# Linear attention and channel mix on one core: a new instruction order, late gate and output tiles in the two-bank PSUM tiles, weight loads as a chain of their own

## The chip, the core and the metric

The kernel runs on one NeuronCore of a Trainium2 chip. The metric is the device time of one execution in microseconds (us). Five runs of the kernel before gave 278.98, 279.91, 278.3, 282.97 and 279.36; their median is 279.36. The profiled execution took 278.98 us, and its span, from the first to the last instruction, is 277.2 us.

Five engines work in parallel, each through its own queue in its own order: PE (matmuls), DVE (vector), ACT (activation functions), POOL (GpSimd) and SP (here only DMA issues). An instruction whose input is not there blocks everything behind it in its engine's queue.

## The reference

Two stages follow each other. The first is a linear attention with a learned feature map, over 8 batches, 8 heads, 576 positions and head dimension 64:

```python
def phi(x):
    proj = einsum('bhsd,df->bhsf', x, w_phi)            # 128 features
    proj = proj - max(abs(proj), axis=-1)
    return concatenate([exp(proj), exp(-proj)], axis=-1)
q_p, k_p = phi(q), phi(k)
kv  = einsum('bhsf,bhsd->bhfd', k_p, v);  z = sum(k_p, axis=2)
num = einsum('bhsf,bhfd->bhsd', q_p, kv)
den = einsum('bhsf,bhf->bhs', q_p, z) + 1e-6
attn = num / den
```

Its output, laid out as 8 x 576 x 512, goes through a channel mix:

```python
x_prev = x shifted by one position (zeros first)
xk = mu_k * x + (1 - mu_k) * x_prev
xr = mu_r * x + (1 - mu_r) * x_prev
k = maximum(xk @ w_k, 0)                                # 512 -> 1024
out = sigmoid(xr @ w_r) * ((k * k) @ w_v)               # 1024 -> 512
```

## The kernel before

**Units of work.** Attention goes by pairs of heads: four pairs in each batch, 32 in all, numbered n = 0 to 31 (pair n belongs to batch n // 4). The channel mix goes by batches b = 0 to 7: the first 512 positions of a batch in `add_moe`, the last 64 positions of two neighbouring batches together in `add_moe_edge`, numbered 0 to 3.

**Steps of a pair** (`add_pair`), each a named operation on one engine:

- `kp`, `qp` (PE, L566) project keys and queries; `rk`, `rq` (DVE, L579 and L584) take the maximum of the absolute values over features.
- `ea`, `eb` (ACT, L605) are the exponentials of the keys; `em` (ACT, L591) those of the maxima; `va`, `vb` (L597, POOL or DVE) scale the values by them.
- `mh`, `mt`, `mc` bring the query maxima into transposed form; `qt` (PE) projects the queries a second time, transposed, and adds the maxima; `qa`, `qb` (ACT, L643) are the exponentials.
- `kv` (PE, L656) sums keys times values, `kc` copies it; `nd` (PE, L677) gives numerator and denominator; `ra`, `rd` (DVE, L685 and L689) divide.
- For pairs 0 to 7 `xt` (PE, L715) transposes the result and `xe`, `xf` copy it; from pair 8 on `xz` does it as a DMA transpose on SP's queue, and `xu` patches the edge.
- `df`, `xa`, `xb` (L726, L732) form the shifted difference and the two mixes xk and xr.

The last 64 positions of each batch go through a smaller set (`add_edge`: `tp`, `rt`, `mhe`, `mte`, `mce`, `qte`, `eme`, `ekt`, `eqe`); `tp` (PE, L466) reads the transposed inputs of all four pairs of its batch.

**Steps of a batch in the channel mix:** `h` (PE, L810, eight per batch, four matmuls each) with `rl` (relu) and `sq` (square); `r` (PE, L829, four per batch) with `th` (tanh, ACT); `v` (PE, L843, four per batch, eight matmuls each) with `ob` (DVE, L849) and `so` (two output DMAs). The edge has `he`, `re`, `ve`, `obe`, `soe`.

An `h` of batch b needs the four `xa` of that batch, an `r` its four `xb`, a `v` all eight `sq` and the weight `w_v`.

**Loads.** Keys and queries of a batch come by `lk` and `lq`, DMAs on POOL's queue that also convert to bf16 (the first pair of batch 0 instead by `hk`, `hq` on SP and ACT, with copies named `lk0.0.d`, `lq0.0.d`). Values come by `lv`, on POOL or SP. In batches 0 and 1 PE transposes keys and queries (`pt`, copied by `pa` and `pb`); from batch 2 on `tr` does it, two DMA transposes per batch on SP's queue (L352), named `tr2.0`, `tr2.2` and so on. The weights come in two DMAs each on POOL's queue: `wk.0`, `wk.1`, `wr.0`, `wr.1`, `wv.0`, `wv.1` (L432). `mus` loads mu_k and mu_r.

**PSUM.** Eight banks are held as three tiles of two banks each (tags P0 to P2, `ptile`) and two tiles of one bank (M0, M1, `motile`). Attention's large results use P tiles. All results of the channel mix and the small transposes use M0 and M1.

**Order.** Every operation is registered with `op(...)`, with its engine, an estimated length, dependencies, and the buffers that it takes and frees. None of these numbers has an effect in this file: the order in which the operations are issued is written out in the string `ORDER`, the result of a planner that ran elsewhere. A word is `name:i/ENGINE+n@t`: `:i` is the PSUM tile, `/ENGINE` the engine where there is a choice, and `+n@t` puts n idle matmuls on a tile of ones ahead of it (`fill`, L292; they compute nothing that is used and keep PE busy). Each engine gets its own operations in the order of this string; waits follow from the data.

Of the kernel before, what the change touches and what calls it, by code (L numbers as in the profile page):

```python
# [19 lines left out]
ones hk hq ident dve2 hk.d hq.d wphi wphi.d lk0.1 lk0.1.d lq0.1 lq0.1.d mus mus.d lk0.2 lk0.2.d dve3  # L20
lq0.2 lq0.2.d lv0.0/POOL lv0.0.d lk0.0.d/DVE lq0.0.d/ACT lv0.1/SP lv0.1.d pt0.0:0+9@0 lv0.2/SP
lv0.2.d pt0.1:1 pa0/DVE pb0/ACT tr0 dve1 tp0.0:0+1@2 kp0:1 rt0.0 qp0:2 rk0 eme0.0 mhe0.0/POOL ekt0.0
pt1.0:1+1@0 lk1.0 lk1.0.d pa1/ACT mte0.0:0 rq0 ea0 lq1.0 lq1.0.d pt1.1:1+2@2 pb1/DVE tr1 lk1.2
lk1.2.d eb0 kp1:2+2@2 tp0.1:0 lq1.2 lq1.2.d rt0.1 em0 rk1 qp1:1+1@1 ekt0.1 mh0/POOL eme0.1 wk.0
wk.0.d mt0:1+1@1 mc0/ACT mce0.0/DVE rq1 ea1 qt0:0+1@2 wk.1 wk.1.d wk.d pt2.0:1 qa0 pt2.1:0
mhe0.1/DVE mh1/POOL pa2/DVE pb2/DVE tr2 eb1 vb0/POOL pt3.0:1+2@3 pt3.1:0 pa3/DVE qb0 pb3/DVE tr3
va0/POOL mte0.1:1+1@3 qp2:2 mt1:0 rq2 qp3:1 mce0.1/ACT mc1/ACT em1 qte0.1:1 wr.0 wr.0.d qt1:0 eqe0.1
qte0.0:0 rq3 lv1.0/POOL lv1.0.d qa1 tp0.2:2 va1/POOL qb1 rt0.2 kp2:1+3@1 rk2 vb1/POOL ekt0.2
kv0:0+1@1 eqe0.0 pt4.0:1 kc0/DVE ea2 mhe0.2/POOL pt4.1:0 pa4/DVE kp3:0 pb4/DVE tr4 kv1:2 wr.1 wr.1.d
wr.d eb2 rk3 pt5.0:0 wv.0 wv.0.d pt5.1:1 eme0.2 qp4:1 pa5/DVE kc1/ACT mh2/POOL em2 rq4 nd0:2  # L30
mh3/POOL pb5/ACT tr5 wv.1 wv.1.d wv.d em3 mt2:0 pt6.0:1 ea3 mc2/DVE ra0 nd1:1 vb2/POOL pa6/DVE rd0
eb3 pt6.1:0 pt7.0:1 va2/POOL pb6/DVE tr6 qt2:2 pa7/ACT ra1 rd1 mte0.2:0 qa2 lk2.0 lk2.0.d pt7.1:1
mce0.2/DVE qp5:0 pb7/DVE tr7 qte0.2:0 lq2.0 lq2.0.d qb2 rq5 tp1.0:1 xt0:1 va3/POOL eqe0.2 kv2:2
rt1.0 xf0/ACT xe0/ACT kp4:0 mh4/POOL mt3:0 kc2/ACT rk4 xt1:1 df0/POOL mc3/ACT ekt1.0 nd2:2 ra2 ea4
vb3/POOL xe1/DVE qt3:1+1@0 rd2 mt4:0 xf1/ACT mc4/ACT df1/DVE qa3 xt2:1 xa0 kv3:2 eb4 mhe1.0/DVE
xe2/DVE mte1.0:0+1@0 xb0 kc3/ACT kp5:0 qb3 qt4:2 xa1 eme1.0 xf2/DVE nd3:1 rk5 mce1.0/ACT df2/POOL
qa4 ra3 qb4 rd3 lv1.2/POOL lv1.2.d ea5 xa2 xt3:0+7@1 qp6:2 xb1 qte1.0:1 xe3/ACT qp7:1 eb5 xf3/DVE
df3/DVE xa3 em4 qt5:0+1@0 eqe1.0 rq6 vb4/POOL h0.0:0 qa5 va4/POOL rq7 kp6:2 qb5 h0.1:1 rk6 mh6/POOL
kp7:1 rl0.1/ACT kv4:0 va5/POOL rl0.0/ACT tr2.0 tr2.0.d tr8 tr9 mt6:1 kc4/DVE ea6 h0.2:0 rk7 vb5/POOL
eb6 xb2 kv5:0+1@2 mc6/ACT sq0.0/ACT xb3 nd4:2 tr2.2 tr2.2.d tr10 tr11 em6 ea7 h0.3:1 kc5/DVE  # L40
vb6/POOL ra4 rd4 nd5:0 eb7 vb7/POOL rl0.3/DVE qt6:2 rl0.2/ACT ra5 qp8:1 rd5 qa6 lv2.0/SP lv2.0.d
sq0.1/POOL r0.0:1 rq8 qb6 va6/POOL qp9:0 h0.4:0 rq9 th0.0 sq0.3/POOL sq0.2/ACT qt7:2 kv6:1 rl0.4/DVE
qa7 lk3.0 lk3.0.d tp2.0:0 kc6/DVE h0.5:1 mh8/POOL rt2.0 qb7 va7/POOL xt4:0 rl0.5/ACT kp8:1 xf4/DVE
xe4/DVE qp10:2 eme2.0 lq3.0 lq3.0.d r0.1:1 rk8 ekt2.0 mhe2.0/POOL r0.2:0 th0.1 rq10 sq0.4/POOL ea8
kp9:0 h0.6:1 rk9 lv2.2/POOL lv2.2.d eb8 kv7:2 th0.2 df4/DVE qp11:1 sq0.5/DVE rl0.6/ACT h0.7:0 xa4
em8 sq0.6/ACT kc7/DVE va8/POOL mt8:1 rq11 rl0.7/ACT nd6:2 mc8/ACT ea9 mte2.0:0 vb8/POOL xt5:1 ra6
nd7:1 rd6 tr3.0 tr3.0.d tr12 tr13 mce2.0/ACT eb9 vb9/POOL qte2.0:0 ra7 kv8:2 rd7 xf5/ACT sq0.7/ACT
qt8:0 va9/POOL kc8/DVE eqe2.0 kp10:1 xe5/DVE kp11:2 rk10 v0.0:1 tr3.2 tr3.2.d tr14 tr15 df5/POOL qa8
rk11 ea10 lk4.0 lk4.0.d v0.1:0 qb8 mh10/DVE xa5 lv3.0/SP lv3.0.d eb10 xb5 kv9:0 xb4 em10 qt9:1
kc9/ACT ob0.0 va10/POOL nd8:0 qa9 ob0.1 v0.2:1 qb9 vb10/POOL ra8 rd8 ea11 lq4.0 lq4.0.d mt10:0  # L50
tp3.0:0 ob0.2 kv10:1 mc10/ACT vb11/POOL eb11 rt3.0 so0.2 so0.2.d xt6:0 xt7:1 kc10/ACT va11/POOL
kp12:2 xf7/ACT xf6/DVE qt10:1 xe6/DVE ekt3.0 xz8 xz8.d xe7/DVE r0.3:0 df6/DVE qa10 rk12 df7/POOL
nd9:0 qb10 v0.3:1 ra9 mhe3.0/POOL rd9 th0.3 xa6 ea12 xz9 xz9.d mte3.0:0 qt11:0 xa7 eb12 nd10:1
mce3.0/DVE ob0.3 tr4.0 tr4.0.d tr16 tr17 h1.0:0 qa11 xb6 h1.1:1 qb11 ra10 xb7 kv11:2 rl1.0/ACT rd10
kp13:0 eme3.0 tr4.2 tr4.2.d tr18 tr19 sq1.0/POOL qte3.0:0 kc11/DVE rl1.1/ACT qp12:1 rk13 qp13:2
# [105 lines left out]
def kernel(  # L161
# [21 lines left out]
    DM = moe_mu_k.shape[0]  # L183
# [36 lines left out]
    op = plan.op  # L220
# [796 lines left out]
```

## Time and profile before

| what | value |
|---|---|
| median of five runs | 279.36 us |
| profiled execution | 278.98 us |
| its span | 277.2 us |
| PE busy | 264.9 us |
| DVE busy | 234.6 us |
| ACT busy | 223.1 us |
| POOL busy | 142.6 us |
| granted TensorE clock | 0.999 |
| DMA | 42.89 MB, mean 155 GB/s |

Busy time is the time in which at least one instruction of the engine was running. For PE the ends of matmuls are modelled and overlap, so its busy time says that matmuls were in flight and not that the array was full. In brackets behind an instruction the profile gives the idle time of its engine before it, and what ended it.

### The profile page before, as it was taken

The page shows a single profiled execution, that of the slowest core. Times are in us where ns is not written, and L with a number is a line of the kernel's source. Part 1 is how long each engine was busy: PE and PEld are TensorE (multiplying, and loading weights), DVE is VectorE, ACT ScalarE, POOL GpSimd, SP SyncE. Part 2 cuts the span into 40 slices and gives each one's busy share as a digit, 9 for nine tenths or more (in the row PEclk, how much of TensorE's full clock was granted, in tenths as well). Part 3 has the DMA queues.
Part 4 walks back from the last instruction along what each step waited for, and adds up shares of the span by engine and source line. Part 5 has one row for each costly group of instructions (what it writes and reads, how often), then busy time and mean ns, then how long its engine had stood idle before and what let it go on. Part 6 is the DMA issues. An engine that isn't in the chain of part 4 may idle for free.

```text
span 277.2 us, 8913 instructions
## 1 busy us (share of the span) xinstructions
PE 264.9 (96%) x3730; PEld 154.3 (56%) x3730; DVE 234.6 (85%) x388; ACT 223.1 (80%) x413; POOL 142.6 (51%) x193
## 2 busy tenths in 40 slices
PE   7999889999599999999999999999999999999993
PEld 3567656565355566555565665555566565444542
DVE  5899999999599989999999889998889797764222
ACT  3899999999599997789898999789987876626330
POOL 6799557976528764534459664830930621300200
PEclk9999999999999999999999999999999999999999
DMA  7999999599999999879799999982635234143034
GB/s 152 269 208 251 208 206 180 124 230 156 214 152 209 199 188 147 180 162 226 92 188 154 193 240 148 184 218 101 144 104 88 64 64 99 35 110 73 22 93 115
DMA packets 65817, 42.89 MB, mean 155 GB/s; under 512 B 47152, under 2 KB 57008, under 8 KB 65776
## 3 DMA queue, kind: packets, MB, share of 16 engines
q1 hardware_dynamic: 54496, 27.54, 49.7%
q0 software_dynamic: 11056, 14.42, 30.3%
q8 instruction: 29, 0.48, 0.7%
q10 hardware_dynamic: 224, 0.36, 0.5%
q14 instruction: 12, 0.10, 0.1%
HBM read 33.62 MB, written 9.44 MB: 155 GB/s over the span
## 4 chain that ended last, share of the span: by engine, by line
PE 81%; DVE 7%; ACT 6%; DMA 4%; issue 1%; SPq 0%; ACTq 0%
PE ps_h L810 20%; PE ps_v L843 18%; PE ps_r L829 10%; PE ps_nd L677 6%; PE ps_kv L656 5%; DMA qkT<-nat 4%; PE ps_he L897 3%; PE ps_k L566 3%; PE ps_ve L929 3%; PE ps_q L566 3%; PE ps_qT L630 2%; PE ps_qT L636 2%; ACT k L605 2%; DVE nmk L579 2%; PE ps_f L292 1%; DVE nmq L584 1%
## 5 line engine op out<-in xcount | busy, mean ns | idle before, releaser
L597 POOL TENSOR_TENSOR v<-vt,v 128x576 bf16<-128x576 f32 x59 | 69.8, 1202 | 30.8 <-ACT v L591 28.4
L605 ACT ACTIVATE k<-ps_k 128x1024 bf16<-128x1024 f32 x64 | 64.8, 1047 | 1.3 <-DVE nmk L579 1.3
L643 ACT ACTIVATE q<-ps_qT 128x1024 bf16<-128x1024 f32 x64 | 63.9, 1054 | 1.8 <-PE ps_qT L636 1.7
L810 PE MATMUL ps_h<-xk,wk_bf 128*128 128x512 bf16 x256 | 61.7, 380 | 0.1
L843 PE MATMUL ps_v<-wv_bf,kk 128*128 128x512 bf16 x256 | 59.0, 379 | 0.0
L579 DVE TENSOR_REDUCE nmk<-ps_k 128x8 f32<-128x1024 f32 x32 | 38.8, 1217 | 1.8 <-PE ps_k L566 1.5
L584 DVE TENSOR_REDUCE nmq<-ps_q 128x8 f32<-128x1024 f32 x32 | 38.3, 1217 | 1.6 <-PE ps_q L566 1.4
L843 PEld LDWEIGHTS <-kk 128*128 128x128 bf16 x256 | 24.1, 98 | 27.3
L810 PEld LDWEIGHTS <-wk_bf 128*128 128x128 bf16 x256 | 22.7, 98 | 25.0 <-issue 0.7
L206 ACT ACTIVATE krelu<-ps_h 128x512 bf16<-128x512 f32 x48 | 28.8, 611 | 9.3 <-PE ps_h L810 9.3
L726 POOL TENSOR_TENSOR diff<-xs 128x576 bf16<-128x576 bf16 x15 | 20.2, 1345 | 30.2 <-ACT xs L706 12.8
L214 POOL TENSOR_TENSOR kk<-krelu 128x512 bf16<-128x512 bf16 x18 | 19.1, 1068 | 30.3 <-ACT krelu L206 26.6
L849 DVE SCALAR_TENSOR_TENSOR ob<-rt,ps_v 128x512 f32<-128x512 bf16 x32 | 21.7, 682 | 14.3 <-PE ps_v L843 13.4
L829 PE MATMUL ps_r<-wr_bf,xr 128*128 128x512 bf16 x128 | 32.0, 380 | 0.0
L732 DVE SCALAR_TENSOR_TENSOR xk<-diff,mu_k_t,xs 128x576 bf16<-128x576 bf16 x32 | 26.7, 839 | 0.1
L835 ACT ACTIVATE rt<-ps_r 128x512 bf16<-128x512 f32 x32 | 19.7, 615 | 8.8 <-PE ps_r L829 8.7
L689 DVE TENSOR_TENSOR x_sc<-ps_nd,rden 128x640 bf16<-128x640 f32 x32 | 26.0, 817 | 0.6
L732 DVE SCALAR_TENSOR_TENSOR xr<-diff,mu_r_t,xs 128x576 bf16<-128x576 bf16 x32 | 25.6, 806 | 0.1
L656 PE MATMUL ps_kv<-v,k 64*128 64x65 bf16 x1024 | 22.5, 190 | 0.3 <-ACT q L643 0.2
L566 PEld LDWEIGHTS <-qkT 64*128 64x128 bf16 x512 | 16.5, 94 | 11.0 <-issue 8.0
L656 PEld LDWEIGHTS <-k 64*128 64x128 bf16 x1024 | 19.3, 94 | 5.7 <-issue 1.8
L677 PE MATMUL ps_nd<-kv,q 128*128 128x65 bf16 x512 | 21.4, 193 | 0.0
(102 smaller groups left out, 415.5 us busy)
## 6 DMA issues: line engine op xcount, KB each, us to landing
out_dram<-ob SPq DMA_DIRECT2D x70, 128.0 KB, 2.5
vt<-in_v_dram SPq DMA_DIRECT2D x11, 576.0 KB, 5.6
nat<-in_k_dram POOLq DMA_DIRECT2D x6, 576.0 KB, 9.2
nat<-in_q_dram POOLq DMA_DIRECT2D x6, 576.0 KB, 9.1
vt<-in_v_dram POOLq DMA_DIRECT2D x4, 576.0 KB, 6.1
wk_bf<-in_moe_w_k_dram POOLq DMA_DIRECT2D x2, 512.0 KB, 12.1
wv_bf<-in_moe_w_v_dram POOLq DMA_DIRECT2D x2, 512.0 KB, 11.1
nat<-in_k_dram POOLq DMA_DIRECT2D x3, 288.0 KB, 7.0
```

Of the source, the lines that this page charges most:

```text
L566: nc.tensor.matmul(ps[:, par, g * 128:(g + 1) * 128], lhsT=qkT[b][r, g0 + gg + g, :], rhs=wph[r, :], start=(g == 0), stop=(g == 3))
L579: nc.vector.tensor_reduce(t[:, j, :], s["k"].rearrange("p a (g f) -> p (a g) f", f=128), axis=AX.X, op=ALU.max, apply_absolute_value=True, ...
L584: nc.vector.tensor_reduce(t[:, j, :], s["q"].rearrange("p a (g f) -> p (a g) f", f=128), axis=AX.X, op=ALU.max, apply_absolute_value=True, ...
L597: (nc.vector if eng == "DVE" else nc.gpsimd).tensor_tensor(vb[:, a, pn, :, 0:64], vt[b, a // 2][:, a % 2, :].rearrange("p (s d) -> p s d", ...
L605: nc.scalar.activation(s[f"k{pn}"], s["k"].rearrange("p a (g f) -> p (a g) f", f=128), AF.Exp, scale=(1.0 if pn == 0 else -1.0))
L643: nc.scalar.activation(t.rearrange("f x (a p) -> f x a p", a=2), s["qT"].rearrange("f a (x p) -> f x a p", p=64), AF.Exp, scale=(1.0 if pn ...
L656: nc.tensor.matmul(ps[:, hh, pn * 65:(pn + 1) * 65], lhsT=s[f"k{pn}"][r, c, :], rhs=vb[r, a, pn, 2 * g + par, :], start=(pn == 0 and c == ...
L677: nc.tensor.matmul(ps[:, bk, o * 65:(o + 1) * 65], lhsT=tail if sl < 2 else s[f"q{pn}"][:, 2 * G + h, :], rhs=s["kv"][:, h, pn, :], start= ...
L732: nc.vector.scalar_tensor_tensor(out=t[:, a, (b % 2) * S:(b % 2 + 1) * S], in0=s["d"], scalar=mu[:, a:a + 1], in1=xs[:, a, 0:S], op0=ALU.m ...
L810: nc.tensor.matmul(ps, lhsT=wk_bf[:, c, fc * 128:(fc + 1) * 128], rhs=xkt[bp][:, c, m0:m0 + 512], start=(c == 0), stop=(c == NDC - 1))
L829: nc.tensor.matmul(ps, lhsT=xrt[bp][:, c, m0 + ci * 128:m0 + (ci + 1) * 128], rhs=wr_bf[:, c, :], start=(c == 0), stop=(c == NDC - 1))
L843: nc.tensor.matmul(ps, lhsT=s["kk"][:, fc, ci * 128:(ci + 1) * 128], rhs=wv_bf[:, fc, :], start=(fc == 0), stop=(fc == NFC - 1))
```

## The change

Three things change in the code, and the string `ORDER` is replaced as a whole.

1. In `add_moe` and `add_moe_edge` the results of `r`, `v`, `re` and `ve` of batches 6 and 7 (and of the last edge) take the first bank of a P tile; for batches 0 to 5 they stay in M0 and M1. `h` and `he` stay in M tiles throughout.

```diff
+    def ntile(key, name):
+        return motile(key, name) if key[0] == "mo" else ptile(key, name)[:, 0, :]
...
+    LATE = 6
...
+        rv = "mo" if b < LATE else "P"
...
-                s["r", ci] = ps = motile(("mo", f"r{b}.{ci}"), "ps_r")
+                s["r", ci] = ps = ntile((rv, f"r{b}.{ci}"), "ps_r")
...
-                s["v", ci] = ps = motile(("mo", f"v{b}.{ci}"), "ps_v")
+                s["v", ci] = ps = ntile((rv, f"v{b}.{ci}"), "ps_v")
```

2. The weight loads get a planner chain of their own; `chain` is not read in this file, and shows only in the order.

```diff
-            op(f"{nm_}.{i}", "POOL", 0.75, i - 8, ldw(...), ["ident"], chain="ld")
+            op(f"{nm_}.{i}", "POOL", 0.75, i - 8, ldw(...), ["ident"], chain="w")
```

3. Of the four output DMAs of the last edge, two instead of one are issued from ACT.

```diff
-                e = "ACT" if hf == 1 and i == 1 else "SP"
+                e = "ACT" if i == 1 else "SP"
```

4. The order. The operations are the same; their places, PSUM tiles and, where there is a choice, engines differ throughout. The places that the prediction speaks of, by engine (before, then after):

```diff
 POOL, from the start
-ident lk0.1 lq0.1 lk0.2 lq0.2 lv0.0 mhe0.0 lk1.0 lq1.0 lk1.2 lq1.2 mh0 wk.0 wk.1 mh1 vb0 va0 wr.0 lv1.0
-va1 vb1 mhe0.2 wr.1 wv.0 mh2 mh3 wv.1 vb2 va2 lk2.0 lq2.0 va3
+ident lv0.1 lk0.1 lq0.1 lk0.2 lq0.2 lv0.2 lk1.0 lq1.0 lk1.2 lq1.2 mhe0.0 wk.0 mh0 va0 vb0 mhe0.1 wk.1
+mh1 lk2.0 mh2 vb1 va1 lv1.0 mhe0.2 lq2.0 wr.0 va2 mh3 vb2 va3 wr.1 vb3
 POOL, around the loads of batch 3
-vb5 vb6 vb7 sq0.1 va6 sq0.3 lk3.0 mh8 va7 lq3.0 mhe2.0 sq0.4 lv2.2
+va5 lk3.0 mh6 vb5 vb6 lq3.0 va6 sq0.2 wv.0 wv.1 vb7 sq0.4 va7
 SP, from the start
-hk wphi mus lv0.1 lv0.2 tr2.0 tr2.2 lv2.0 tr3.0 tr3.2 lv3.0
+hk lv0.0 wphi mus tr2.0 lv1.2 tr2.2 lv2.0 tr3.0 tr3.2 lv2.2 xz8 lv3.0
 DVE, from the start
-ones dve2 dve3 lk0.0.d pa0 dve1 rt0.0 rk0 rq0 pb1 rt0.1 rk1 mce0.0 rq1 mhe0.1 pa2 pb2 pa3 pb3 rq2
+ones dve2 dve3 lq0.0.d pa0 dve1 rt0.0 rk0 pa1 rq0 rk1 mc0 rq1 pa2 pb2 rt0.1 pa3 rq2 pb3 rk2
 PE, the last words
-h7.7 he3.0 v6.3 v7.0 he3.1 r7.2 r7.3 v7.1 v7.2 v7.3 re3 ve3.0 ve3.1
+h7.7 r6.3 r7.0 he3.0 r7.1 r7.2 v7.0 he3.1 v7.1 r7.3 v7.2 v7.3 re3 ve3.0 ve3.1
 output DMAs at the end
-SP: soe3.0.a soe3.0.b soe3.1.a          ACT: soe3.1.b
+SP: soe3.1.a soe3.0.a                   ACT: soe3.0.b soe3.1.b
 idle matmuls in all
-36
+30
```

Between the first `h` of batch 0 (`h0.0`) and the first of batch 1 (`h1.0`) PE's list holds the same operations as before and four more: `kp13`, `qp12`, `kv11` and `qte3.0`, which before stood behind `h1.0`.

## The prediction

> **What bounds the kernel now.** I read the busy time by stage first, cut at the moments that the order makes important: the last `xa` of batch 0 (39.9), the first long wait (69), the start of `h1.0` (80.3), the last matmul (273). Columns: stage, length, then busy time of PE, PEld, DVE, ACT and POOL with instruction counts, clock, DMA share, GB/s.
>
> ```profile
> 0.00:39.90 39.90, 35.27 (x561) 22.65 (x562) 35.59 (x77) 34.02 (x75) 29.11 (x50) 1.00 1.10 221
> 39.90:69.00 29.10, 28.43 (x525) 17.32 (x526) 28.82 (x43) 28.61 (x51) 23.56 (x28) 1.00 0.98 167
> 69.00:80.30 11.30, 8.50 (x142) 5.28 (x141) 8.10 (x16) 8.49 (x14) 5.88 (x7) 1.00 1.29 204
> 80.30:273.00 192.70, 192.67 (x2510) 109.07 (x2506) 161.67 (x254) 151.95 (x277) 84.05 (x110) 1.00 0.71 138
> ```
>
> Two regimes: up to 80 DVE and ACT are the full engines (in the second stage DVE idles 0.28 us); from 80.3 PE has 0.03 us of gaps in 192.7, so nothing that frees a buffer there can gain. The stage between shows a hole on every engine. The chain of waits names it (start, length, what):
>
> ```profile
> 63.73 9.78 DMA qkT<-nat
> 73.51 0.05 issue
> 73.56 0.29 PE ps_e L466 x4
> ```
>
> `tp3.0` needs both DMA transposes of batch 3; `tr3.2`, issued at 63.73, lands 9.78 later. PE queues `kv10`, `xt6`, `kp12` behind it. DVE's timeline shows the cost, and where it idles early (idle time in brackets):
>
> ```profile
> 6.26 0.49 DVE L202 COPY qkT<-ps_pt 128x640 bf16<-128x640 bf16 x1 [1.39 <-PE ps_pt L338]
> 7.42 0.42 DVE L472 TENSOR_REDUCE me<-ps_e 128x2 f32<-128x256 f32 x1 [0.53 <-PE ps_e L466]
> 73.89 1.23 DVE L472 TENSOR_REDUCE me<-ps_e 128x8 f32<-128x1024 f32 x1 [2.67 <-PE ps_e L466]
> ```
>
> `h1.0` starts at 80.34, 0.33 after `xa7` ends on DVE (80.01). So the path is: DVE from the start to `xa7`, then PE to 272.97, then 4.22 of output to 277.19; outside the span the execution has 278.98 - 277.19 = 1.8.
>
> **The change, part by part.**
>
> *Start on DVE.* DVE is busy 35.59 of the 39.90 up to `xa3`, so 4.3 idle, nearly all before 16 us. In the new order its list up to `xa3` has the same reductions and mixes. Small copies change engine: `pa1`, `pa7`, `pb5`, `kc2`, `xe0`, `df2` and five shorter ones come (3.2 us), `pb1`, `xe1`, `xe2`, `df1`, `mhe0.1`, `mhe1.0` and five shorter ones go (3.0; 0.36 to 0.40 for a PSUM copy, 0.30 for a pair of small ones, start to start in the trace): 35.9. What changes is the idle time. Two value loads of 288 KB now go out ahead of keys and queries: `lv0.0` in SP's queue before `wphi` and `mus`, `lv0.1` in POOL's before `lk0.1`, `lq0.1`, `lk0.2`, `lq0.2`. In the trace these four land at 5.33, 6.87, 9.26 and 12.36; the first two are 1.55 apart for 288 KB. Lower bound of the delay: 0, if the values move before POOL's first packets (3.9 us). Upper: 2 x 1.55 = 3.1. I take one load, 1.55, halfway, because `lv0.1` stands in front of the keys in the same queue, while `lv0.0` follows `hk` (landed 4.39) in a queue that then carries only the small `wphi` and `mus`. `lq0.2` then lands at 13.9, `pt2.0` (five transposes, 0.45, and two hand-overs of 0.1) lets `pa2` start at 14.6. DVE's work ahead of `pa2` sums to 9.6 (three 1.13 reductions, 1.13 for `rk0`, 5.1 of set-up and copies), so idle is 5.0, with the bounds 3.5 and 6.5. `wphi` behind `lv0.0` delays `dve1` and `rk0` by up to 1; that lies inside the same idle time, since `pa2` waits anyway. `xa3` ends at 35.9 + 5.0 = 40.9 (39.4 to 42.4), against 39.90.
>
> POOL now issues ten loads in a row (about 0.75 each in the rows of its issues) before `mhe0.0`, which moves from 7.91 to 9.0; behind it `mte0.0`, `mce0.0` and then all of ACT's exponentials wait, `ea0` by 1.3. I cost this at nothing: ACT's list up to `qb5` is 2.0 shorter than before (32.7 against 34.7), and `qb3`, which feeds DVE's `ra3`, comes at 31 while DVE reaches `ra3` at 35. Without that cover it would be 1.3.
>
> [...]
>
> *Middle on DVE.* From `xa3` to `xa7` DVE needed 80.01 - 39.90 = 40.1: 36.3 of work, 2.67 + 0.42 in the hole, 0.7 in small gaps. The new list has 2.0 more work before `xa7` (`ob0.3` 0.60, `ra10` + `rd10` 0.95, `sq0.0`, `sq0.3`, `sq0.6` 1.02, small ones; less `rl0.4`, two copies of kv and others). `lk3.0` and `lq3.0` pass `vb5`, `vb6`, `vb7`, `sq`, `va7` on POOL (1.1 us each) and so go out some 7 us earlier; before they were issued at 51.8 and 54.2 and landed 5.8 and 6.3 later. With `lq3.0` issued at 47 and landed by 54, `tr3.2` is issued by 57 and lands, at the same 9.8, by 67; `tp3.0` is reached at about 67. I take the hole as gone, bounds 0 and 3.1 left. `lv2.2` now waits in SP's queue behind `tr3.2`: issued at 60 instead of 56.4, at its 6.8 it lands at 67, when POOL reaches `va10` (67.4 before), so nothing. `lk2.0` and `lq2.0` too come earlier, but before nothing waited for `tr2`: nothing. So `xa7` ends at 40.9 + 38.3 + 0.7 = 79.9. PE has cover for this: its work from `h0.0` to `h1.0` is 32.9 before and 34.2 now (the four operations moved ahead), and in the 40.5 it took before, 3.0 were the hole and 4.6 losses, so it needs 38.8 of the 39.1 there are. `h1.0` starts at 80.0.
>
> *The end on PE.* Before, `h1.0` to the last matmul took 192.6: 184.4 at the shortest start-to-start times of each operation (`h`, `r` 0.863, `v` 1.726, `nd` 0.635, `kv` 0.555, `qt` 0.43, `kp`, `qp` 0.233) and 8.2 on top. Of that 6.9 are 68 changes between 64-row and 128-row matmuls at 0.1 each. The new order leaves 183.0 behind `h1.0` and has 66 changes: 191.1 with the rest unchanged. Last matmul at 271.1; bounds of new stalls 0 to 3, taken 0, since DVE's list runs some 4 us ahead of PE at `h3.0` by the sums of both.
>
> *P tiles for the last `r` and `v`.* The last stretch before:
>
> ```profile
> 251.09 6.95 PE ps_h L810 x32
> 258.04 0.89 PE ps_he L897 x16
> 258.93 3.45 PE ps_v L843 x16
> ```
>
> 32 matmuls in 6.95 are 217 ns each, the same as in a single group: with two M tiles nothing waits. The matmuls are the same, so gain 0 (at most 0.6, all of the excess after 240), loss at most 1 where the new `h7.0`, now ahead of `v6.0`, meets `xa31`, which by DVE's list ends about 1 us before it.
>
> *Idle matmuls.* Six fewer (0.45 each in the first nine): PE waits there for DVE in any case, so 0; 2.7 at most if it did not.
>
> *Output at the end.* SP issues `soe3.0.a` after `soe3.1.a`, 0.54 each, both behind `obe3.1`; ACT takes one more. Last issue at 1.1 instead of 0.95 after `obe3.1`: +0.2, so 4.4.
>
> Sum: 271.1 + 4.4 + 1.8 = **277.3 us**, 0.6% under the profiled execution (278.98) and 0.7% under the median (279.36).
>
> [...]
>
> **The rivals.**
>
> *A. The late weights take the place of the hole (slower).* `wv.0` and `wv.1` move on POOL from 21 and 23 us to behind `lq3.0` and `sq0.2`, about 51. The six weight rows land 8.9 to 13.0 after issue: 60 to 64.4. `v0.0` comes on PE at 40.9 + 19.2 + 3.7 = 63.8. If POOL, which before waited up to 7.6 for ACT ahead of a `va` or `vb`, reaches `wv.1` 4 later, it lands at 68.4, and `v0.0`, with `kp11`, `v0.1`, `tp3.0` behind it, loses 4.6: 281.9. It decides the sign once `wv.1` lands 3.5 after `v0.0`'s turn. Against it: DMA is less full there (share 0.98, against 1.10 early).
>
> *B. The start keeps what the middle gives (no change).* Both value loads in full and some more early waits: idle 7.5 instead of 5.0, 279.8. For it: DMA share 1.10 up to 40. Against it: most of the first 4 us of the queues are open.
>
> *C. The new order stalls PE after 80.* Ten hand-overs of 0.2 to 0.3 that the old order did not have: 2.5, 279.8. For it: every neighbour in the queues is new. Against it: DVE and ACT are idle for 31 and 41 us in that stage.
>
> **How the numbers follow.** Forecast 0.50, A 0.18, B 0.18, C 0.14. The forecast's own range is 275.8 to 278.9 (idle 3.5 to 6.5). Up to 0.5% either way (277.96 to 280.76) cannot be told from no change. Faster: 0.46 from the forecast, 0.02 each from B and C: 0.50. Slower: 0.15 from A, 0.04 from B, 0.05 from C: 0.24. Same: 0.26. The range is 275.6 to 281.0: below it 0.05, above it 0.14, most of A.
>
> **What would show it.** Right: no DMA wait at `tp3.0`, `h1.0` at 79 to 81.5, PE without gaps from there, 191 us to its last matmul. The start is read at `xa3` (40.9) and in DVE's idle time before `pa2`. Wrong: a wait of `v0.0` on `wv`, `xa3` after 43, PE gaps above 0.3 after 85, or the 9.8 of `tr3.2` back in the chain.

## The result and the profile after

| what | before | after |
|---|---|---|
| median of all runs, us | 281.08 (80 runs) | 281.26 (43 runs) |
| ratio after / before, 95% interval | | 1.0082 [1.0065, 1.0100] |
| profiled execution, us | 278.98 | 281.12 |
| its span, us | 277.2 | 279.3 |
| `xa3` ends | 39.90 | 41.27 |
| `xa7` ends | 80.01 | 83.29 |
| `h1.0` starts | 80.34 | 83.33 |
| last matmul ends | 272.97 | 275.01 |
| DVE standing still behind POOL ahead of `h1.0` (see below) | 0.00 | 3.94 |

The change made the kernel 0.8% slower; the forecast was 277.3 us, 0.6% faster. The ratio leaves out, for each kernel, the runs more than 1.5% above its fastest (in the changed kernel at a mean granted clock of 0.982 to 0.990, the others at 0.984 to 1.0), and the medians hold them, which is why the two medians lie so close.

The stages first, cut at the same events as before: end of `xa3`, 69, start of `h1.0`, last matmul (columns as in the prediction).

```profile
0.00:41.27 41.27, 32.69 (x558) 21.40 (x559) 36.63 (x75) 33.56 (x73) 30.17 (x53) 1.00 1.07 210
41.27:69.00 27.73, 25.54 (x489) 15.45 (x488) 27.06 (x42) 25.93 (x45) 22.42 (x27) 1.00 1.05 181
69.00:83.30 14.30, 12.88 (x235) 8.07 (x233) 14.20 (x24) 12.66 (x20) 8.48 (x6) 1.00 0.93 179
83.30:275.00 191.70, 190.88 (x2450) 107.68 (x2446) 161.67 (x246) 151.54 (x276) 83.59 (x112) 1.00 0.71 137
```

The hole of the third stage is gone: DVE is busy 14.20 of 14.30 us, where it had 8.10 of 11.30. Yet the first three stages together are 3.0 us longer. So DVE was kept busy and had more to be busy with; but 24 instructions in 14.20 us (0.59 each) against 16 in 8.10 (0.51) suggests that some of them became longer. DVE's timeline of after shows which (start, length, engine, line, operation; from the loads on, its line numbers are 3 to 6 higher than in before).

```profile
69.04 0.81 DVE L736 SCALAR_TENSOR_TENSOR xk<-diff,mu_k_t,xs 128x576 bf16<-128x576 bf16 x1
70.50 1.77 DVE L736 SCALAR_TENSOR_TENSOR xk<-diff,mu_k_t,xs 128x576 bf16<-128x576 bf16 x1
72.79 1.21 DVE L475 TENSOR_REDUCE me<-ps_e 128x8 f32<-128x1024 f32 x1
75.60 0.81 DVE L736 SCALAR_TENSOR_TENSOR xr<-diff,mu_r_t,xs 128x576 bf16<-128x576 bf16 x1
76.33 1.24 DVE L483 CAST mhlt<-me 128x4 bf16<-128x4 f32 x1
```

The reduction at 72.79 is `rt3.0`; it carries no bracket, so the 2.67 us of idle time before it are gone, as forecast. But `xa5` at 70.50 takes 1.77 us, the same instruction as `xa4` at 69.04 with 0.81, and the 4-column cast of `mhe3.0` takes 1.24 us, where `mhe2.0`, the same cast on DVE at 56.89, takes 0.16. POOL's timeline beside them:

```profile
70.49 3.93 POOL L601 TENSOR_TENSOR v<-vt,v 128x576 bf16<-128x576 f32 x3 [1.62 <-ACT v L595]
75.90 1.65 POOL L730 TENSOR_TENSOR diff<-xs 128x576 bf16<-128x576 bf16 x1 [1.47 <-issue]
```

POOL's `va10` began at 70.49, 0.01 us ahead of `xa5`, and lasted to 71.65; `xa5` ended 0.62 later. `df6` ran from 75.90, and the cast did not end until it had. A busy time that contains standing still looks like work: no idle time and no releaser is shown for it. Only the length of an instruction against that of its like shows it. The chain of waits of after, which begins with the late load of `wphi`, goes through all four such places (start, length, what):

```profile
2.28 5.38 DMA wph_f<-in_w_phi_dram
...
38.82 2.45 DVE xk L736 x2
...
47.37 2.37 DVE xr L736 x2
...
69.13 0.73 DVE xk L736
...
70.58 1.69 DVE xk L736
...
76.41 1.17 DVE mhlt L483
```

The first pair is `xa2` and `xa3`, the second `xb2` and `xb3`; two undisturbed ones take 1.46 here (0.73 each). What each lost beyond its usual length: `xa3` 0.99, `xb3` 0.91, `xa5` 0.96, `mhe3.0` 1.08, between them 3.94 us ahead of `h1.0`. In the profile of before no DVE instruction ahead of `h1.0` is longer than its like. From 78.81 on the chain runs on PE, through `v0.3` and the operations that moved ahead of `h1.0`, so PE comes to `h1.0` just when `xa7` ends.

A fifth such place lies behind `h1.0`. DVE's, POOL's and PE's timelines:

```profile
115.64 1.50 DVE L214 TENSOR_TENSOR kke<-krelu 128x512 bf16<-128x512 bf16 x1
```

```profile
115.14 1.72 POOL L730 TENSOR_TENSOR diff<-xs 128x576 bf16<-128x576 bf16 x1 [5.42 <-DVE xr L736]
```

```profile
117.87 1.02 PE L815 MATMUL ps_h<-xk,wk_bf 128*128 128x512 bf16 x4 [0.82 <-DVE ob L854]
```

`sqe0.0`, a square whose like on DVE at 271.37 took 0.42 us, took 1.50 beside `df12` on POOL. `ob1.3` behind it came late, and `h2.1` on PE waited 0.82 us for the M tile that `ob1.3` frees.

The end, on PE's timeline (its ends overlap, so starts are compared):

```profile
257.50 1.89 PE L815 MATMUL ps_h<-xk,wk_bf 128*128 128x512 bf16 x8
259.22 1.89 PE L834 MATMUL ps_r<-wr_bf,xr 128*128 128x512 bf16 x8
260.95 1.06 PE L903 MATMUL ps_he<-xk,wk_bf 128*128 128x128 bf16 x16
```

Eight `h` matmuls from 257.50 to 259.22 are 215 ns each, eight `r` to 260.95 are 216: nothing waits for a PSUM tile here.

### The profile page after: what moved, and what is told of

Same layout as the page of the kernel before. It is cut to its first block, busy times and chain, and to the rows that moved or that the text cites. A ratio compares the mean times of both kernels' runs of the same rounds, so it can differ in the third digit from the quotient of the medians.

```text
span 279.3 us, 8899 instructions
## 1 busy us (share of the span) xinstructions
PE 262.0 (94%) x3724; PEld 152.6 (55%) x3724; DVE 240.0 (86%) x385; ACT 223.7 (80%) x410; POOL 144.7 (52%) x197
## 4 chain that ended last, share of the span: by engine, by line
PE 75%; DVE 17%; ACT 4%; DMA 2%; issue 1%; SPq 1%; DVEq 0%; ACTq 0%
PE ps_v L848 19%; PE ps_h L815 18%; PE ps_r L834 9%; PE ps_nd L681 6%; PE ps_kv L660 5%; DVE nmq L588 4%; DVE nmk L583 3%; PE ps_he L903 3%; PE ps_ve L935 3%; PE ps_k L570 2%; PE ps_q L570 2%; PE ps_qT L634 2%; DMA wph_f<-in_w_phi_dram 2%; PE ps_qT L640 2%; DVE xk L736 2%; ACT k L609 2%
## 5 line engine op out<-in xcount | busy, mean ns | idle before, releaser
L601 POOL TENSOR_TENSOR v<-vt,v 128x576 bf16<-128x576 f32 x56 | 66.1, 1201 | 22.5 <-ACT v L595 22.5
L609 ACT ACTIVATE k<-ps_k 128x1024 bf16<-128x1024 f32 x64 | 63.8, 1031 | 1.8 <-DVE nmk L583 1.8
L815 PE MATMUL ps_h<-xk,wk_bf 128*128 128x512 bf16 x256 | 63.1, 380 | 0.8 <-DVE ob L854 0.8
L647 ACT ACTIVATE q<-ps_qT 128x1024 bf16<-128x1024 f32 x64 | 63.2, 1038 | 0.8 <-PE ps_qT L640 0.4
L730 POOL TENSOR_TENSOR diff<-xs 128x576 bf16<-128x576 bf16 x18 | 26.1, 1453 | 32.0 <-DVE xr L736 16.4
L214 POOL TENSOR_TENSOR kk<-krelu 128x512 bf16<-128x512 bf16 x17 | 18.0, 1061 | 34.9 <-ACT krelu L206 17.7
L206 ACT ACTIVATE krelu<-ps_h 128x512 bf16<-128x512 f32 x37 | 22.0, 601 | 8.3 <-PE ps_h L815 6.9
L736 DVE SCALAR_TENSOR_TENSOR xk<-diff,mu_k_t,xs 128x576 bf16<-128x576 bf16 x32 | 27.8, 875 | 0.1
L736 DVE SCALAR_TENSOR_TENSOR xr<-diff,mu_r_t,xs 128x576 bf16<-128x576 bf16 x32 | 26.9, 845 | 0.0
L212 ACT ACTIVATE kk<-krelu 128x512 bf16<-128x512 bf16 x33 | 20.7, 633 | 7.5 <-DVE krelu L208 7.3
L208 DVE TENSOR_SCALAR krelu<-ps_h 128x512 bf16<-128x512 f32 x27 | 18.3, 686 | 6.7 <-PE ps_h L815 4.7
```

What stands on the lines that cost most here:

```text
L601: (nc.vector if eng == "DVE" else nc.gpsimd).tensor_tensor(vb[:, a, pn, :, 0:64], vt[b, a // 2][:, a % 2, :].rearrange("p (s d) -> p s d", ...
L609: nc.scalar.activation(s[f"k{pn}"], s["k"].rearrange("p a (g f) -> p (a g) f", f=128), AF.Exp, scale=(1.0 if pn == 0 else -1.0))
L647: nc.scalar.activation(t.rearrange("f x (a p) -> f x a p", a=2), s["qT"].rearrange("f a (x p) -> f x a p", p=64), AF.Exp, scale=(1.0 if pn ...
L736: nc.vector.scalar_tensor_tensor(out=t[:, a, (b % 2) * S:(b % 2 + 1) * S], in0=s["d"], scalar=mu[:, a:a + 1], in1=xs[:, a, 0:S], op0=ALU.m ...
L815: nc.tensor.matmul(ps, lhsT=wk_bf[:, c, fc * 128:(fc + 1) * 128], rhs=xkt[bp][:, c, m0:m0 + 512], start=(c == 0), stop=(c == NDC - 1))
```

## The experiments

Theory 1: a DVE instruction that reads its inputs from SBUF stands still while POOL works on SBUF, and the new order made four such meetings on DVE's path to `xa7`. Rival 2: the extra DVE work and the later start set `xa7`. Rival 3: the shared P tiles cost the time. Each kernel was compared with runs of the kernel before on the same chip; the edits below are moves within an engine's list, except where it is said.

### The four meetings moved apart

```diff
 ACT
-em4 qb4      ea7 behind em6      em10 eb11
+qb4 em4      em6 behind ea7      eb11 em10
 mhe3.0
-DVE
+POOL, behind vb11
```

> Theory 1 (four DVE instructions before h1.0 stood still behind a POOL instruction that reads SBUF: xa3 +1.0, xb3 +0.9, xa5 +1.0, mhe3.0 +1.1, together 4.0 us): with em4, em6 and em10 one place later on ACT, so that va4, vb6 and va10 start after the DVE instruction, and mhe3.0 on POOL, h1.0 starts 3 to 4 us earlier than the changed kernel's 83.3 and the time falls by 2.5 to 3.5 us. Rival 2 (the 2.0 us of DVE work that was moved ahead of xa7, and the late start, set the time; DVE would have waited in any case): h1.0 at 82.5 or later, time within 0.8 us of the changed kernel.

282.97 us median of 6 runs, ratio 1.0118 [1.0032, 1.0204]: not faster. All four meetings are gone (`xa3` ends at 39.76, 1.5 earlier), but a new one came. DVE's timeline of this kernel, then POOL's:

```profile
54.38 4.60 DVE L214 TENSOR_TENSOR kk<-krelu 128x512 bf16<-128x512 bf16 x1
```

```profile
54.34 1.19 POOL L601 TENSOR_TENSOR v<-vt,v 128x576 bf16<-128x576 f32 x1
55.48 1.05 POOL L214 TENSOR_TENSOR kk<-krelu 128x512 bf16<-128x512 bf16 x1
56.48 1.17 POOL L601 TENSOR_TENSOR v<-vt,v 128x576 bf16<-128x576 f32 x1
57.60 1.03 POOL L214 TENSOR_TENSOR kk<-krelu 128x512 bf16<-128x512 bf16 x1
```

`sq0.3`, 0.41 us long in the changed kernel, now takes 4.60: it starts 0.04 behind POOL's `vb7` and ends only as the first four of a back-to-back train are through, some 4.2 us late. With `sq0.6` (0.75) DVE stood still for some 4.9 us, more than before the edit, and `xa7` ended at 84.99. (This profiled execution also ran at half the TensorE clock from 35.9 to 39.3 and from 59.8 to 63.2.) The mechanism shows more strongly than in the change itself; as a removal the experiment failed.

### Two meetings put into the kernel before

```diff
 ACT
-qb4 ea5 xe3 eb5 em4
+qb4 em4 ea5 xe3 eb5
```

> The kernel before with one word moved: em4 ahead of ea5 on ACT, so that vb4 and va4 on POOL run while DVE does xb1, df3 and xa3. Theory 1: one to two DVE instructions there take about 1 us longer, xa3 ends at 41 to 42 instead of 39.9, and the time rises by 0.8 to 2 us. Rival 2: every DVE instruction keeps its length, time within 0.5 us of before.

`vb4` and `va4` now run beside `xb1` and `df3`: 0.91 and 0.75 us longer, and `xa3` ends at 41.34 instead of 39.90, as Theory 1 has it. The whole time, 285.7 us median of 10 runs and ratio 1.0144 [1.0018, 1.0269], is too wide to price them: the profiled execution also ran at half the clock for 6.8 us, from 77.1, in the hole at `tp3.0` (more on that below). The eleventh run repeats the edit on a kernel without the hole.

### The code of the change with the order of before

```diff
-r6.0:0
+r6.0:1
```

That is the only word of the order that differs; the P tiles and the output queue are those of the change.

> All code of the change (P tiles for r and v of batches 6 and 7, one more output DMA on ACT) with the order of before. Both theories, and the prediction's step on the P tiles: nothing, within 0.3 us of before. Rival 3 (the P tiles themselves cost): slower by 1 us or more, with gaps on PE after 240.

286.73 us median of 6 runs (279.46 to 289.58), too scattered for a ratio. By the profile nothing stands still ahead of `h1.0`, `xa3` ends at 39.79, and `h1.0` to the last matmul takes 193.15 us against 192.63. All of the 0.52 arises at `r6.0` (0.18) and `r6.1` (0.33), the first results in P tiles: they cost 0.5 in the old order.

### `wphi` ahead of the values

```diff
 SP
-hk lv0.0 wphi mus
+hk wphi mus lv0.0
```

> The changed kernel with lv0.0 behind wphi and mus in SP's queue. dve1 no longer waits 1.57 us for wphi, rk0 starts about 1.1 earlier. Rival 2 in its form of a late start: xa3 and h1.0 about 1.1 earlier and the time 0.8 to 1.2 us lower. Theory 1: all of DVE shifts, so which instructions meet changes; the gain is 1.1 less what new meetings cost, and h1.0 is 79.4 plus the sum of the meetings before it, plus or minus 0.7, less 1.1.

282.59 us median of 12 runs, ratio 1.0076 [1.0011, 1.0141], no gain. `rk0` starts at 7.88 instead of 8.66, but `lq0.2` lands at 14.22 instead of 12.60, `pa2` waits, and `xa3` ends at 41.81 instead of 41.27, without any meeting ahead of it. Part of that is the clock, which was at half from 14.5 to 17.9 in this profiled execution. The late `wphi` by itself is not tested cleanly here, since the edit also brought `lq0.2` later; the eighth run comes back to it. A new wait shows on POOL's timeline:

```profile
76.27 3.43 POOL L601 TENSOR_TENSOR v<-vt,v 128x576 bf16<-128x576 f32 x3 [7.78 <-DMA vt<-in_v_dram]
```

`lv2.2`, behind `tr3.2` in SP's queue, lands too late for `va10`. In the changed kernel it landed at 70.18, 0.31 before `va10` began.

### The early loads alone, too early

```diff
 POOL
-lv1.2 vb4 va4 ... sq0.3 lk3.0 mh8 va7 lq3.0 mhe2.0
+lv1.2 lk3.0 lq3.0 vb4 va4 ... sq0.3 mh8 va7 mhe2.0
```

> The kernel before, with the loads lk3.0 and lq3.0 moved up on POOL right behind lv1.2, into an idle stretch at 37 us (they stood at 51.8 and 54.2 us); nothing else. This isolates the one gain that the change did bring, the hole before rt3.0 (2.67 us of DVE's time before). Theory 1 (the change took out this hole and lost more by vector instructions standing still behind POOL): without the other reorderings the hole is gone, tr3.0 is issued by 53 us instead of 60.6, no DVE instruction ahead of h1.0 is longer than usual, h1.0 starts at 77.3 to 78.3 us, the last matmul ends at about 270 to 271 us, and the time falls by 2 to 3 us against the kernel before (ratio 0.989 to 0.993). Rival (the hole was hidden anyway, another wait takes its place): h1.0 stays within 0.5 us of 80.3 and the time within 0.3% of the kernel before.

280.24 us median of 12 runs, ratio 1.0038 [0.9982, 1.0093]. The hole before `rt3.0` is gone and nothing stands still, but `xa7` ends at 81.04. SP's timeline of the kernel before, and of this one:

```profile
40.37 6.54 SPq L352 DMA_TRANSPOSE qkT<-nat  x2
```

```profile
40.00 11.63 SPq L352 DMA_TRANSPOSE qkT<-nat  x2
```

The two transposes of batch 2 now run while `lk3.0` and `lq3.0` are on their way (landed at 44.1 and 49.1), and `tr2.0` lands at 50.9 instead of 47.0, `tr2.2` at 54.5 instead of 48.8. DVE's timeline:

```profile
51.58 1.23 DVE L584 TENSOR_REDUCE nmq<-ps_q 128x8 f32<-128x1024 f32 x1 [2.49 <-PE ps_q L566]
53.95 1.23 DVE L584 TENSOR_REDUCE nmq<-ps_q 128x8 f32<-128x1024 f32 x1 [1.14 <-PE ps_q L566]
```

`rq8` and `rq9` wait 3.6 us for `qp8` and `qp9`. PE stood idle for 2.71 us until `tr2.0` had landed and `qp8` could start at 50.93; then the clock was at 0.51 from 50.3 to 53.8, in which `r0.0` took 1.89 us instead of 1.03. This is the rival's case: the hole was moved forward, not removed.

### The meetings apart, and the squares on ACT

```diff
 the first experiment, and
 sq0.3, sq0.6
-DVE
+ACT
```

> The first experiment again (em4, em6 and em10 a few places later on ACT, mhe3.0 on POOL), and sq0.3 and sq0.6, on which DVE stood still there for 4.18 and 0.75 us, on ACT instead. Theory 1: DVE is blocked by at most 1.0 us ahead of h1.0 (3.95 in the changed kernel), xa7 ends at 79.5 to 80.8 us instead of 83.3, h1.0 starts at 79.6 to 81 us, the stretch from h1.0 to the last matmul stays at 191.5 to 191.9, the last matmul ends at 271.2 to 272.7 us, and the time is 2.3 to 3.8 us under the changed kernel's profiled 281.1. Rival 2 (DVE's extra work and the late start set xa7): the blocking goes, but xa7 still ends at 82 us or later, and the last matmul at 274 us or later.

283.27 us median of 12 runs, ratio 1.0182 [1.0115, 1.0249]. The standing still falls to 1.79 us (`df4` 0.91, `xb4` 0.88), yet `xa7` ends at 86.43. POOL's timeline has the cause that the fourth experiment showed:

```profile
75.14 3.93 POOL L601 TENSOR_TENSOR v<-vt,v 128x576 bf16<-128x576 f32 x3 [7.87 <-DMA vt<-in_v_dram]
```

POOL came earlier to `lk4.0` (64.48, in the changed kernel 66.06), ahead of `lv2.2` (66.40, in the changed kernel 65.39), and `lv2.2` took 8.6 us to land instead of 4.8. That the order of the two is the reason is read from their times and was not tried by itself. Neither theory is decided by this run.

### The early loads with the code of the change

> The order of the fifth experiment with the code of the change: gate and output results of batches 6 and 7 in P tiles, two of the last output transfers from ACT; only r6.0's tile number differs. Theory 1 (P tiles cost nothing): the profile ahead of h6.0 agrees with the fifth experiment within 0.3 us, no PE gap over 0.5 us behind 240 us, last matmul within 0.6 us and the time within 0.4% of the fifth experiment. Rival 3 (the shared P tiles make late batches wait and cost the 2 us): the last matmul ends 1.5 to 2.5 us later than in the fifth experiment, with gaps before r6, v6, r7 or v7.

The order of the fifth experiment on the code of the change, `r6.0` on the other tile. 280.81 us median of 12 runs, ratio 1.0004 [0.9955, 1.0052]; the medians differ by 0.57, the ratios the other way, within their intervals. In this profiled execution the clock was at half for 6.8 us from 50.2, in the fifth for 3.4, so the times ahead of `h1.0` can't be compared. From `h1.0` to the last matmul it takes 193.28 us against 192.63 in the fifth: 0.65 more, of which 0.53 arises at `r6.0` and `r6.1` as in the third experiment and the rest before 115 us. The one wait behind 224 us on PE's timeline:

```profile
244.05 1.04 PE L834 MATMUL ps_r<-wr_bf,xr 128*128 128x512 bf16 x4 [0.16 <-DVE x_sc L693]
```

This is `r6.1`, which waits until DVE has read the P tile that `nd31` left. Rival 3 in its full size falls; a cost of some 0.5 us in the old order stays.

### The start of before in the changed order

```diff
 the sixth experiment, and
 SP
-hk lv0.0 wphi mus
+hk wphi mus lv0.1 lv0.2
 POOL
-ident lv0.1 lk0.1 lq0.1 lk0.2 lq0.2 lv0.2
+ident lk0.1 lq0.1 lk0.2 lq0.2 lv0.0
```

> The sixth experiment with the loads of the start as in the kernel before: lk0.1, lq0.1, lk0.2, lq0.2 and then lv0.0 on POOL, wphi and mus and then lv0.1 and lv0.2 on SP; everything else as in the sixth. If the late wphi costs what it shows (dve1 at 7.76 us instead of 6.67): dve1 at 6.6 to 6.9, rk0 at 7.7 to 7.9, lq0.2 landed by 12.4, xa3 ends 0.7 to 1.0 us ahead of the sixth experiment's (about 38.9 instead of 39.8), h1.0 at 78.8 to 80.2, the time 0.2 to 0.4% under the sixth's. If the gain is taken back at pa2, as in the fourth experiment: xa3 within 0.3 us of the sixth's, and the same time.

284.62 us median of 6 runs, ratio 1.0162 [1.0059, 1.0264]. `dve1` starts at 6.50 instead of 7.83 and `pa2` at 12.64 instead of 13.78, and `xa3` still ends at 40.08 (40.02): DVE waits 1.07 us ahead of `rq3` instead. So the start gives nothing back. And in the sixth experiment, with the late start but no meeting ahead of `xa3`, `xa3` ends at 40.02, only 0.12 later than in the kernel before. With that the start half of Rival 2 falls.

### Meetings apart, values in time

```diff
 the sixth experiment, and
 DVE
-rt2.0 df4 mhe2.0 kc6 rk8 rq11 rk9
+rt2.0 kc6 rk8 rq11 rk9 df4 mhe2.0
 SP
-lv2.0 tr3.0 tr3.2 lv2.2
+lv2.0 lv2.2 tr3.0 tr3.2
```

> The sixth experiment, in which df4 and xb4 still stood still behind POOL (1.79 us) and lv2.2 landed so late that va10 waited 7.9 us, with three more moves: df4 and mhe2.0 behind rk9 on DVE, where POOL pauses, and lv2.2 on SP ahead of tr3.0 instead of behind tr3.2. Theory 1 (the changed kernel's middle is long because DVE stands still behind POOL, and nothing else): blocked at most 0.9 us ahead of h1.0, no wait of va10 for its values, DVE gaps of 1.5 us at most between xa3 and xa7, xa7 ends at 79.5 to 81.5 us (83.3 in the changed kernel), h1.0 at 79.6 to 82, the last matmul at 271.2 to 273.5 us and a ratio to the kernel before 0.006 or more below the changed kernel's 1.0082. Rival 2 (extra work and late start set xa7): xa7 at 82.5 us or later though nothing is blocked and no transfer is late, last matmul at 274.5 us or later.

279.68 us median of 12 runs, ratio 1.0036 [0.9994, 1.0079], the changed kernel's being 1.0082 [1.0065, 1.0100]: by the middle values about half the loss is back, less than Theory 1 asked for, and the intervals overlap. `va10` no longer waits, DVE stands still for 0.88 us instead of 3.94, `xa7` ends at 82.51 (Rival 2's bound was 82.5), the last matmul at 274.23 (its bound was 274.5). Its profiled execution has one disturbance, shown by the busy time by stage:

```profile
33.00:36.60 3.60, 2.18 (x40) 1.31 (x34) 3.34 (x8) 3.36 (x10) 2.14 (x3) 1.00 1.06 145
36.60:40.00 3.40, 3.40 (x31) 2.14 (x31) 3.40 (x7) 3.40 (x6) 0.00 (x0) 0.50 0.97 207
```

At half the clock for 3.4 us PE came to `h0.0` at 41.85 (40.75 in the changed kernel), and DVE's idle time between `xa3` and `xa7` rises from 0.78 to 3.44. How much of this the clock made, and how much PE as the next bound (the prediction left it 0.3 us of room), this run doesn't tell.

### The early loads, placed behind the transposes

```diff
 POOL
-vb5 vb6 vb7 sq0.1 va6 sq0.3 lk3.0 mh8 va7 lq3.0
+vb5 lk3.0 lq3.0 vb6 vb7 sq0.1 va6 sq0.3 mh8 va7
```

> The kernel before, with lk3.0 and lq3.0 on POOL right behind vb5 (45 to 46.4 us, idle in the profile of before) instead of at 51.8 and 54.2 us: later than in the fifth experiment, where they went ahead of tr2.0 and tr2.2 and pushed these from 47.0 and 48.8 to 50.9 and 54.5 us. If transposes wait for the loads issued ahead of them and nothing else was wrong there: tr2.0 and tr2.2 land as before (47 to 49.5 us), tr3.0 is issued by 56 and tr3.2 landed by 69 us, the hole before rt3.0 is gone, no other gap over 1 us and no blocked DVE instruction ahead of h1.0, h1.0 at 77.2 to 78.6 us, last matmul at 270 to 271.5, ratio 0.990 to 0.995. Rival (the hole is worth nothing): last matmul at 272.5 us or later although the hole is gone.

276.51 us median of 12 runs (275.57 to 277.74), ratio 0.9932 [0.9900, 0.9965]: faster than both kernels. `tr2.2` landed at 52.0, later than expected, though nothing waited for it; `tr3.2` landed at 67.2 instead of 73.5. The stages, cut at `xa3`, 69, `h1.0` and the last matmul:

```profile
0.00:39.94 39.94, 34.97 (x558) 22.70 (x562) 35.72 (x77) 34.02 (x75) 28.89 (x50) 1.00 1.10 219
39.94:69.00 29.06, 28.03 (x517) 17.32 (x526) 28.79 (x43) 28.57 (x52) 23.35 (x27) 1.00 1.10 198
69.00:77.54 8.54, 8.43 (x142) 5.33 (x143) 8.04 (x16) 8.50 (x15) 5.98 (x8) 1.00 1.05 180
77.54:270.17 192.63, 190.64 (x2473) 109.02 (x2505) 161.61 (x254) 151.97 (x277) 84.11 (x110) 1.00 0.70 137
```

Only the third stage differs in length from the kernel before: 8.54 us instead of 11.30, with the same 16 DVE instructions in 8.04. The last matmul ends 2.8 us earlier. So the hole was worth nearly what the prediction had put on it (3.1), if nothing else is changed.

### One meeting on top of it

```diff
 ACT
-qb4 ea5 xe3 eb5 em4
+qb4 em4 ea5 xe3 eb5
```

> The kernel of the run ahead of this one with em4 ahead of ea5 on ACT, as in the second experiment, so that vb4 and va4 on POOL run beside xb1 and df3 on DVE. Theory 1 (a DVE instruction with two inputs in SBUF stands still until POOL's ends, and what it loses goes on to h1.0): xb1 and df3 lose 1.5 to 1.8 us together, xa3 ends 1.3 to 1.7 us later, h1.0 1.0 to 1.7 us later, last matmul 0.8 to 1.7 us later, ratio 0.003 to 0.006 higher. Rival (time lost ahead of xa3 is taken back by slack before h1.0): h1.0 and the last matmul within 0.4 us of the run ahead of it, though xa3 is late.

277.71 us median of 12 runs, ratio 0.9979 [0.9939, 1.0019]: 1.20 us and 0.0047 more. DVE's timeline without the meeting, then with it:

```profile
37.68 0.81 DVE L732 SCALAR_TENSOR_TENSOR xr<-diff,mu_r_t,xs 128x576 bf16<-128x576 bf16 x1
...
38.62 0.46 DVE L726 TENSOR_TENSOR diff<-xs 128x576 bf16<-128x576 bf16 x1
```

```profile
37.43 1.72 DVE L732 SCALAR_TENSOR_TENSOR xr<-diff,mu_r_t,xs 128x576 bf16<-128x576 bf16 x1
39.08 0.18 DVE L202 COPY xs<-ps_x 128x63 bf16<-128x63 bf16 x1
39.29 1.21 DVE L726 TENSOR_TENSOR diff<-xs 128x576 bf16<-128x576 bf16 x1
```

`xb1` and `df3` lose 1.66 us; the copy between them, whose input is in PSUM, has its 0.18 in both. `xa3` ends 1.41 later, `xa7` and `h1.0` 1.36 later, the last matmul 1.80 (0.4 of it arose behind `h1.0`). No slack on the way takes it up.

### A second meeting, late in the middle

```diff
 ACT
-qb8 eb10 em10
+qb8 em10 eb10
```

> The kernel of the meeting built into the early loads (em4 ahead of ea5, loads behind vb5), and a second meeting: em10 ahead of eb10 on ACT, so that va10 and vb10 start on POOL at about 67 instead of 68 us, while DVE has xb5 and xb4. It doubles the suspected cost, at a second place, late in the middle, as in the changed kernel. Theory 1: xb5 or xb4 takes 1.6 to 2.0 us instead of 0.81 (up to 3 if it waits for both POOL instructions), the blocked time ahead of h1.0 goes from 1.66 to 2.5 to 3.0 us, xa7 ends at 79.3 to 80.2 us (78.6 with the first meeting alone, 77.2 with none), h1.0 at 81.3 to 82.4, the last matmul at 272.5 to 273.5, and the ratio to the kernel before is 1.000 to 1.005 (0.9979 and 0.9932). Rival (late in the middle DVE has slack that takes it up): xb4 is late but xa7 and the last matmul stay within 0.3 us of the kernel with the first meeting alone.

278.84 us median of 12 runs, 1.13 above the run ahead of it, which was taken on another chip. `va10` now runs beside `xb4`, which takes 0.91 longer, so DVE stands still for 2.57 us; `xa7` ends at 79.86, the last matmul at 272.82, both as Theory 1 had them. `h1.0` starts at 80.19, 1.3 later than with one meeting; the expectation was set too late, from a start that I had misread, since some matmul records are missing there. The ratio, 0.9923 [0.9880, 0.9966], missed. It rests on 17 runs of the kernel before, none under 278.4, against 276.84 beside the run ahead (and 276.82 on this same chip beside the first four experiments), so it isn't set against the others.

## Why the prediction was wrong

Term by term, in us:

| term | predicted | measured |
|---|---|---|
| start to end of `xa3` | 40.9 | 41.27 |
| `xa3` to end of `xa7` | 39.0 | 42.02 |
| `xa7` to `h1.0` | 0.1 | 0.04 |
| `h1.0` to the last matmul | 191.1 | 191.68 |
| last matmul to the end of the span | 4.4 | 4.3 |
| outside the span | 1.8 | 1.8 |
| sum | 277.3 | 281.1 |

**The step that failed** is "So `xa7` ends at 40.9 + 38.3 + 0.7 = 79.9". It priced every DVE instruction as in the trace of before, in whatever company it would run on POOL. Measured, the middle is 38.29 of work (predicted 38.3), 0.78 of gaps (0.7), and 2.95 of standing still, for which the sum had no term and the rivals no case. With the 0.99 inside the start it is 3.94, slightly more than the whole miss of 3.8; the other terms nearly cancel. (The prediction's starting figures for the middle, 36.3 of work and 0.7 of small gaps, are 36.63 and 0.39 by the profile's busy time; their sum is right.) The extra work that Rival 2 names is real, but it was in the sum.

The price of such time is shown: 0, 1.66 and 2.57 us of it in three otherwise equal kernels gave a last matmul at 270.17, 271.96 (0.4 of it from elsewhere) and 272.82, about 1.03 us for each us, and medians of 276.51 and 277.71 on one chip and 278.84 on another. That removing the 3.94 from the changed order would bring them all back is not shown: the one run that took 3.06 of them out without a late transfer returned about half the loss by its middle value, with a disturbed profile.

Of the mechanism the runs show which instructions grew, and by how much. `xa5`, second by 0.01 us, lost 0.96; the cast of `mhe3.0` lost 1.08, so the "two inputs" of my expectations was too narrow. In the changed kernel no copy out of PSUM on DVE took more than 0.49 us and no key or query reduction more than 1.23; two of these reductions ran from 41.19 beside POOL's train of 39.49 to 43.42 and took 2.34 us together. Why DVE stands still beside POOL is not shown.

**The start** (40.9, measured 41.27) was near by luck, through two errors. `lq0.2` landed at 12.60, not 13.9, so the values ahead of the keys cost 0.24 and not 1.55, and `pa2` started at 13.71, not 14.6. Idle time up to `xa3` was 4.64 (5.0 predicted) and work 35.64 (35.9); in the place of the difference came 0.99 of standing still. That the later `wphi` lies inside the idle time held in effect: taking it away twice did not move `xa3` forward.

**POOL's ten issues** stood in the sum at nothing and were not quite free: `mhe0.0` came at 8.82 (9.0 predicted), `ea0` 1.7 later (1.3), and DVE waited 0.56 us at `ra3`, where the chain of waits comes from ACT's exponentials. The cover of 4 us that the sum had there did not last.

**The hole** went, as said: `tr3.2` landed at 67.28 (67 predicted), and `tp3.0` found it there. The time was right by luck: `tr3.2` was issued at 61.98, not 57, and landed in 5.30 us, not 9.8. Its worth was nearly right (2.8 us in the kernel that only moves the two loads).

**`lv2.2`** cost nothing, but by 0.31 us, and again by two errors (issued at 65.39, not 60, landed in 4.79 us, not 6.8); two experiments that came to `va10` sooner, or to `lk4.0` sooner, lost some 7.8 us of POOL's time there.

**The end on PE** was 0.6 longer than said, and still 0.95 shorter than before. The 0.82 of waiting at `h2.1`, taken as 0 in the sum, is more than that excess, and it is the same failed step: `sqe0.0` stood still behind POOL. In the eighth run, where `sqe0.0` met nothing, PE did not wait there and the stretch took 190.75 us. P tiles showed no wait in the new order; in the old one they cost 0.5, inside the bound of 1.

**The rivals.** A did not come: `wv.1` was issued at 52.8 and landed at 61.89, and `v0.0` ran at 64.96 without a wait for it. B gave nearly the time but not the cause: `xa3` ended 1.4 later than before, where B needed 3.5. C did not come in its size: instead of ten small hand-overs PE had one wait of 0.82 us (a gap above 0.3 behind 85 us, which the prediction had named as a sign of being wrong).

## What to carry to other kernels

When an order is changed, do not take an instruction's length from the old trace without its company: list the DVE instructions with inputs in SBUF that come to lie beside POOL's, and give each some 0.9 us (here), more where POOL runs a train; then compare lengths of like instructions, since standing still is counted as busy. A load that comes too late is best moved alone and only as far as its own stretch allows: the same two loads brought 2.8 us behind the transposes of the batch before and nothing ahead of them. Where an order lives on margins of 0.3 us, taking one stall out can cost more than it gives, so remove stalls one at a time and look at the next late transfer.

## What the runs showed of the hardware

**One waiting instruction missed four turns.** In the first experiment `sq0.3` did not get in between POOL's instructions, which followed each other without a pause, but stood still for four of them, 4.2 us; in the changed kernel `xa5`, behind the first of three, lost 0.96 and got in before the second was through.

**The TensorE clock fell to half for 3.4 or 6.8 us at a time.** In the third experiment, busy time by stage around the hole at `tp3.0` (the third value from the end of a line is the clock):

```profile
71.05:74.71 3.66, 0.00 (x1) 0.00 (x0) 0.45 (x1) 1.16 (x3) 2.36 (x3) 1.00 1.41 125
74.71:81.53 6.82, 3.45 (x64) 2.89 (x66) 2.39 (x5) 1.23 (x4) 0.07 (x1) 0.50 1.15 229
```

PE did nothing for 3.66 us and then ran at 0.50 for 6.8 us. But the clock also fell where PE had not been idle for so long: in the ninth run (its lines stand there) PE was busy for 2.18 of the 3.6 us ahead of the drop, 61%, and so idle for 1.42 us in all; the clock was then at 0.50 for 3.4 us. What sets a drop off is not shown. In the tenth run, without the hole, the mean clock stayed at 0.996 or above in all 12 runs, and their times within 2.2 us.
